# A retention whose carried state drops its padding and sits on four quarters of the array, with the first weight fetched a unit later

## The chip, the cores and the metric

One core of one Trainium2 chip runs the whole program. The metric is the device time of one execution in microseconds (us). The kernel before takes 575.39 us, the median of 3 runs (574.91 to 575.91). Everything is float32 in the results; the matrix products of the two MLPs are made of float32r pieces.

## The reference

Retention over 2 batches, 8 heads, 768 tokens and 64 columns a head, in blocks of 64 tokens with a state that decays; its result (1536 tokens by 512) goes through two MLPs of 512 to 2048 to 512, the first with a squared ReLU, the second with a leaky one. The weights come as 64-bit floats.

```
for b in range(nb):
    intra = (qb @ kb.T * Dmask) @ vb
    inter = (qb * lam_pow) @ kv_state
    out[sl] = intra + inter
    kv_state = lam_block * kv_state + (kb * rev_pow).T @ vb
h = np.maximum(x @ w_in, 0.0);  x = (h * h) @ w_out
h = x @ w_in2;  out = np.maximum(0.01 * h, h) @ w_out2
```

## The kernel before, in words

**Retention.** It works in units of 128 tokens: 2 batches of 6 chunks make 12 units, numbered 0 to 11. The 8 heads are 4 pairs p of two heads (par 0 and 1). A unit has these steps. `transposes` turns k and q by TensorE (L294), and ScalarE copies them out as kT and qT (L298). `scale_q` makes qS on VectorE (L304). `scores` multiplies kT by qT on the two row halves of the array, par 0 into one bank and par 1 into another (L311). `mask` multiplies with the decay table into Pm (L316). `state` scales k on GpSimd to kd (L329), multiplies by v (L335) and adds the old state times its decay (L342 on GpSimd, L347 on VectorE). `output` adds qS times the old state (L360) and Pm times v (L362) in one bank, and `split` takes this apart into xhi (ScalarE, L68) and xlo (VectorE, L69), the MLP's input. The tile of the state is 128 by 4 by 128: the two heads of a pair are two 64 by 64 blocks on the diagonal, with zeros beside them, so L360 contracts over 128 rows and writes 64.

**Order.** In this part the orders of TensorE and of SP, which issues the loads, are as the code is written; the scheduler places the other engines' work. The loop at the end of `retention` does for unit i: transposes of unit i+2, loads of k and q of unit i+4 and of v of unit i+2, then state and output of i, mask of i+1, scores of i+2. k has 5 buffers, q and v have 3 each.

**Weights.** A piece of weights (1 MB of 64-bit numbers, tile raw) is fetched by `fetch` and turned into float32r hi and lo in steps by `converting`: one on ScalarE (L114, the absolute value of the high words), the others on VectorE, to w1h (ScalarE, L135) and w1l (VectorE, L137). The first is fetched at i = 1 and converted one step in each of units 3 to 9.

**MLPs.** Four stages each, 64 us to the end. Two stages of the first MLP, (0,1) and (0,2), have their second layer for two token tiles as seven products instead of eight (`second_pair`, L503 in the profile like all products of the MLPs). Parts of it, P1, P6 and P67, are kept in DRAM by `keep`: written by SP in stage (0,1), added by GpSimd's DMAs in stage (0,2). After stage (0,2), ten DMAs from DRAM to DRAM (L684) add them up into `spill`, which the last stage reads.

Of the kernel before, what the change touches and what calls it, by code (L numbers as in the profile page):

```python
# [15 lines left out]
P = 128  # L16
# [3 lines left out]
def tile_retention_then_two_mlps(  # L20
# [43 lines left out]
    def dma(dst, src):  # L64
        return nc.sync.dma_start(dst, src)  # L65
# [7 lines left out]
    def source(l, s, n, h):  # L73
        w = ((w1, w2), (w3, w4))[l][n]
        if n == 0:
            return w[:, s * FS + h * CW:s * FS + (h + 1) * CW].rearrange("(k p) f -> p k f", p=P)
        return w[s * FS + h * CW:s * FS + (h + 1) * CW, :].rearrange("(k p) f -> p k f", p=P)

    order = [(0, 0, 0, 0), (0, 0, 0, 1), (0, 0, 1, 0), (0, 0, 1, 1)]
    stages = [(l, s) for l in range(2) for s in range(NS)]  # L80
    for before, stage in zip(stages, stages[1:]):
# [8 lines left out]
    def fetch():  # L90
        if todo:
            key = todo.pop(0)
            r = raw.tile([P, 4 * CW], I64, tag="raw", name="raw")
            k = 4 if key[2] == 0 else 2
            dma(r.rearrange("p (k f) -> p k f", k=k), source(*key))
            fetched.append((key, r))

    def converting():
# [85 lines left out]
    def retention(ctx_att, att):  # L184
# [90 lines left out]
                DTr[:, par], bass.AP(tensor=row.tensor, offset=row.offset, ap=[[1, P], [2 * W, NP], [1, C]])))  # L275

        def column_of_powers():
            ps = bank()[:, 0:H]
            nc.tensor.transpose(ps, pw[:, 1:C + 1], ident[0:H, 0:H])
            nc.scalar.copy(kdec, ps)  # L280

# [35 lines left out]

        st = []
        for e in range(2):
            st.append(att.tile([P, NP, P], F32, name=f"st{e}"))  # L320
            nc.gpsimd.memset(st[e], 0.0)

        def state(n):
            b, c = units[n]
            if c == NCH - 1:
                return
            kn, vn = nats[n, "k"], nats[n, "v"]
            kd = wk.tile([P, NP, 2, D], F32, tag="kd", name="kd")
            nc.gpsimd.tensor_tensor(  # L329
                out=kd, in0=kn.rearrange("s (a r) d -> s a r d", r=2),  # L330
                in1=kdec.rearrange("s (a r o) -> s a r o", r=2, o=1).to_broadcast([P, NP, 2, D]), op=ALU.mult)
            ps = bank()[:, 0:NP * D].rearrange("p (a e) -> p a e", a=NP)
            for p in range(NP):
                for par in range(2):
                    nc.tensor.matmul(ps[par * D:(par + 1) * D, p, :], kd[:, p, par, :], vn[:, 2 * p + par, :],  # L335
                                     start=True, stop=True)
            old, new = st[c % 2], st[(c + 1) % 2]
            if c:
                tmp = wk.tile([P, NP, D], F32, tag="tmp", name="tmp")
                for par in range(2):  # L340
                    r = slice(par * D, (par + 1) * D)
                    nc.gpsimd.tensor_tensor(out=tmp[r], in0=old[r, :, r],  # L342
                                            in1=LR[r, :, C - 1:C].to_broadcast([D, NP, D]), op=ALU.mult)
            for par in range(2):
                r = slice(par * D, (par + 1) * D)
                if c:
                    nc.vector.tensor_tensor(out=new[r, :, r], in0=ps[r], in1=tmp[r], op=ALU.add)  # L347
                else:
                    nc.vector.tensor_copy(new[r, :, r], ps[r])

        def output(n):
            b, c = units[n]
            vn = nats[n, "v"]
            ps = bank().rearrange("p (a s) -> p a s", a=NP)
            for p in range(NP):

                rows = [slice(par * D, (par + 1) * D) for par in range(2)]
                if c:
                    for r in rows:
                        nc.tensor.matmul(ps[r, p, :], st[c % 2][:, p, r], qS[n][:, p, :], start=True, stop=False)  # L360
                for par, r in enumerate(rows):
                    nc.tensor.matmul(ps[r, p, :], vn[:, 2 * p + par, :], Pm[n][:, par, p, :], start=c == 0, stop=True)  # L362
            t, o = divmod(b * S + c * C, TT)
            if xhi[t] is None:
                new_x(t)
            split(xhi[t][:, :, o:o + C], xlo[t][:, :, o:o + C], ps)

        n_units = len(units)
        FILL = TT // C
# [11 lines left out]
        rows_of_powers()  # L381
        scale_q(1, q1)
        scores(1)
        state(0)
        mask(0)
        output(0)
        scale_q(2, transposes(2))
        state(1)
        mask(1)
        scores(2)  # L390
        for i in range(n_units):
            if i and i + 2 < n_units:
                scale_q(i + 2, transposes(i + 2))
            if i + 4 < n_units:
                load(i + 4, "kq")
            if i + 2 < n_units:
                load(i + 2, "v")
            if i in (1, 9):
                fetch()
            if i:  # L400
                if i > 1:
                    state(i)
                output(i)
                if i + 1 < n_units:
                    mask(i + 1)
                if i + 2 < n_units:
                    scores(i + 2)
            if 3 <= i <= 9:
                convert(pin=True)


# [190 lines left out]
            put(h, r22[h], r22[h], 1, 1)  # L602
            put(h, s2[h], s2[h], 0, 1)

    partial = [{n: dram.tile([P, TT], F32, name=f"partial{p}{n}") for n in ("P1", "P6", "P67")} for p in range(2)]

    def keep(src, dst, first):
        f = plain()
# [6 lines left out]


    def second_pair(s):
        begun = (0, s - 1) in seven
        (g0h, g0l), (g1h, g1l) = g[0], g[1]
        x = {  # L620
            "B11": [(g0h[:, 2 * h], g0l[:, 2 * h]) for h in range(2)],
            "B21": [(g0h[:, 2 * h + 1], g0l[:, 2 * h + 1]) for h in range(2)],
            "B22": [(g1h[:, 2 * h + 1], g1l[:, 2 * h + 1]) for h in range(2)],
            "T1": [(g1h[:, 2 * h], g1l[:, 2 * h]) for h in range(2)],
            "T2": [(tt[2][:, 0, h], tt[2][:, 1, h]) for h in range(2)],
        }
        ps = {}

        def product(p, where, a, b, start=True):
            if start:  # L630
                ps[p, where] = bank()
            ops = []
            for h in range(2):
                if a[0] == "A":
                    i, j = int(a[1]) - 1, int(a[2]) - 1
                    hi, lo = (w[:, j, (2 * p + i) * P:(2 * p + i + 1) * P] for w in wts[0, s, 1, h])
                else:
                    hi, lo = (sums[0, s, 1, h][:, part, int(a[1]) - 1, p] for part in range(2))
                bh, bl = x[b][h]
                ops += [(hi, bh), (hi, bl), (lo, bh)]  # L640
            three(ps[p, where], ops, start, True, not start)
            return ps[p, where]

        def kept(p, i, k):
            return spill[0][k][2 * p + i]

        def late_split(n, old, m):
            x[n] = x[old]
            with tc.high_priority(offset=400):
                for h in range(2):  # L650
                    split(*x[n][h], later[m(h)])

        both = range(2)
        for p in both:
            keep(product(p, "A", "A11", "B11"), partial[p]["P1"], not begun)
            yield True
        for p in both:
            keep(product(p, "C", "S1", "T1"), kept(p, 1, 1), False)
            yield True
        late_split("T3", "T1", lambda h: (1, 2 * h))  # L660
        for p in both:
            keep(product(p, "A", "A12", "B21", False), kept(p, 0, 0), False)
            yield True
        late_split("T4", "B21", lambda h: (0, 2 * h + 1))
        for p in both:
            keep(product(p, "C", "S4", "B22", False), kept(p, 0, 1), False)
            yield True
        for p in both:
            keep(product(p, "B", "S2", "T2"), partial[p]["P6"], not begun)
            yield True  # L670
        for p in both:
            keep(product(p, "D", "A22", "T4"), kept(p, 1, 0), False)
            yield True
        yield from first(0, s, 2)
        for p in both:
            keep(product(p, "B", "S3", "T3", False), partial[p]["P67"], not begun)
            yield True
        opened.add(("sums", 0, s + 1))
        if (0, s + 1) not in seven:
            for p in both:  # L680
                p1, p6, p67 = (partial[p][n] for n in ("P1", "P6", "P67"))
                for dst, src in ((p67, p1), (kept(p, 0, 1), p1), (kept(p, 0, 1), p6), (kept(p, 1, 0), p67),
                                 (kept(p, 1, 1), p67)):
                    nc.gpsimd.dma_start(dst, src, accum_op=ALU.add, max_dma_last_dim=TT)  # L684

    def second(l, s, t, ms=range(4)):
        last = s == NS - 1
# [94 lines left out]
```

## Time and profile before

| what | us |
|---|---|
| median of 3 runs | 575.39 |
| the profiled execution, whole | 576.42 |
| its span, first to last instruction | 574.5 |
| TensorE busy in the span | 564.2 |
| VectorE busy | 418.4 |
| ScalarE busy | 305.0 |
| GpSimd busy | 83.9 |

The profiled execution took 1.92 us outside the span, and 1.03 us more than the median. Retention fills the first 64 us, the MLPs the rest. TensorE's orders are written out, so its idle time is what an order or a neighbour costs. All rows name the kernel's lines.

### The profile page before, as it was taken

Reading aid. Unit: us, or ns where it says so; the run is one execution under the profiler, and the core shown is the slowest. Engines: PE = TensorE matmul, PEld = TensorE weight load, DVE = VectorE, ACT = ScalarE, POOL = GpSimd, SP = SyncE. Lnnn points to the kernel's source line nnn. Section 1 sums busy time; section 2 is a strip of 40 time slices with the busy share of each in tenths; the row PEclk is TensorE's granted clock in tenths of the full one; section 3 lists DMA queues with packets and bytes.
Section 4 is the critical chain, followed back from the end, with each engine's and each line's share of the span. In section 5 each row is a group of like instructions: output and inputs, shape, how many; then the busy total and the mean of one; then the engine's idle time right before and its main releaser. Section 6 shows DMA issues by size and latency. Waiting matters only on the chain.

```text
span 574.5 us, 8051 instructions
## 1 busy us (share of the span) xinstructions
PE 564.2 (98%) x3075; PEld 470.7 (82%) x3075; DVE 418.4 (73%) x589; ACT 305.0 (53%) x477; POOL 83.9 (15%) x101
## 2 busy tenths in 40 slices
PE   7989999999999999999999999999999999999997
PEld 6878888888788888888888888888888888888886
DVE  3879999999927599498478999929873996217222
ACT  2344598546757687758448374553562376225110
POOL 3426000000040105445000000000203011310000
PEclk9999999999999999999999999999999999999999
DMA  8997434665492649999713216341529523661432
GB/s 172 239 213 177 156 121 138 234 183 180 172 164 57 73 148 181 203 249 189 185 36 91 76 41 216 128 165 74 103 55 246 109 29 47 76 90 56 162 113 92
DMA packets 74071, 78.12 MB, mean 136 GB/s; under 512 B 40105, under 2 KB 46513, under 8 KB 74033
## 3 DMA queue, kind: packets, MB, share of 16 engines
q1 hardware_dynamic: 60448, 60.57, 34.6%
q0 software_dynamic: 13056, 16.78, 20.9%
q8 instruction: 24, 0.39, 0.3%
q10 hardware_dynamic: 528, 0.26, 0.2%
q14 instruction: 15, 0.11, 0.1%
HBM read 52.43 MB, written 27.80 MB: 140 GB/s over the span
## 4 chain that ended last, share of the span: by engine, by line
PE 74%; DVE 15%; DMA 6%; issue 3%; SPq 1%; ACT 1%; POOL 0%; DVEq 0%; POOLq 0%; ACTq 0%
PE ps L503 72%; DMA raw<-in_moe_w_in 2%; DVE rb L122 2%; DMA raw<-in_moe_w_out 2%; DVE hb L125 2%; DVE hb L118 2%; SPq L65 1%; DVE rb L121 1%; DVE hb L115 1%; DVE Pm L316 1%; DMA k<-in_k 1%; DVE xlo L69 1%; DVE w1l L137 0%; DVE g1l L474 0%; DVE sw L442 0%
## 5 line engine op out<-in xcount | busy, mean ns | idle before, releaser
L503 PE MATMUL ps<-xhi,w1h 128*128 128x512 f32 x288 | 112.1, 389 | 0.0
L503 PE MATMUL ps<-xlo,w1h 128*128 128x512 f32 x288 | 112.0, 389 | 0.0
L503 PE MATMUL ps<-xhi,w1l 128*128 128x512 f32 x288 | 112.0, 389 | 0.0
L613 POOL DMA_DIRECT2D spill<-f x48 | 46.9, 1047 | 347.6 <-ACT f L609 347.5
L609 ACT COPY f<-ps 128x512 f32<-128x512 f32 x84 | 48.9, 586 | 74.1 <-PE ps L503 72.7
L503 PEld LDWEIGHTS ps<-xhi,w1h 128*128 128x128 f32 x288 | 54.1, 188 | 11.3 <-issue 0.2
L503 PEld LDWEIGHTS ps<-xlo,w1h 128*128 128x128 f32 x288 | 54.1, 188 | 11.3
L503 PEld LDWEIGHTS ps<-xhi,w1l 128*128 128x128 f32 x288 | 54.1, 188 | 11.2
L474 DVE TENSOR_TENSOR g0l<-f,g0h 128x512 fp32r<-128x512 f32 x52 | 35.1, 687 | 33.7 <-ACT f L470 22.1
L503 PE MATMUL ps<-w2l,g0h 128*128 128x512 f32 (+1 forms) x132 | 50.5, 383 | 0.0
L503 PE MATMUL ps<-w2h,g0l 128*128 128x512 f32 (+1 forms) x132 | 50.5, 383 | 0.0
L503 PE MATMUL ps<-w2h,g0h 128*128 128x512 f32 (+1 forms) x132 | 50.5, 383 | 0.0
L137 DVE TENSOR_TENSOR w2l<-hb,w2h 128x1024 fp32r<-128x1024 f32 x16 | 19.5, 1222 | 39.8 <-ACT w2h L135 39.8
L114 ACT ACTIVATE hb<-raw 128x1024 f32<-128x1024 f32 x32 | 36.8, 1150 | 19.2 <-DVE w2l L137 7.4
L503 PE MATMUL ps<-g0h,w2h 128*128 128x512 f32 x104 | 40.5, 389 | 0.0
L503 PE MATMUL ps<-g0l,w2h 128*128 128x512 f32 x104 | 40.5, 389 | 0.0
L503 PE MATMUL ps<-g0h,w2l 128*128 128x512 f32 x104 | 40.5, 389 | 0.0
L122 DVE SCALAR_TENSOR_TENSOR rb<-raw,rb 128x1024 f32<-128x1024 uint32 x32 | 39.1, 1221 | 0.4
L125 DVE TENSOR_TENSOR hb<-hb,rb 128x1024 f32<-128x1024 f32 x32 | 39.1, 1220 | 0.4
L118 DVE SCALAR_TENSOR_TENSOR hb<-raw,hb 128x1024 uint32<-128x1024 uint32 x32 | 39.1, 1220 | 0.3
L567 DVE TENSOR_TENSOR f<-ps,f 128x512 f32<-128x512 f32 x40 | 26.2, 684 | 9.9 <-PE ps L503 9.9
L714 DVE TENSOR_TENSOR f<-ps,f 128x512 f32<-128x512 f32 (+1 forms) x25 | 16.7, 669 | 22.9 <-PE ps L503 21.7
(141 smaller groups left out, 1139.4 us busy)
## 6 DMA issues: line engine op xcount, KB each, us to landing
raw<-in_moe_w_in SPq DMA_DIRECT2D x16, 1024.0 KB, 5.6
raw<-in_moe_w_out SPq DMA_DIRECT2D x16, 1024.0 KB, 5.0
spill<-f POOLq DMA_DIRECT2D x48, 256.0 KB, 4.8
spill<-f SPq DMA_DIRECT2D x24, 256.0 KB, 2.6
f<-spill SPq DMA_DIRECT2D x24, 256.0 KB, 2.9
k<-in_k SPq DMA_DIRECT2D x12, 256.0 KB, 4.9
q<-in_q SPq DMA_DIRECT2D x12, 256.0 KB, 5.1
v<-in_v SPq DMA_DIRECT2D x12, 256.0 KB, 4.8
```

The costliest lines, as they stand in the source:

```text
L65: return nc.sync.dma_start(dst, src)
L114: nc.scalar.activation(hf, w_hi.bitcast(F32), AF.Abs)
L118: yield ve.scalar_tensor_tensor(out=hb, in0=w_hi, scalar=0xC0000000, in1=hb, op0=ALU.bitwise_and, op1=ALU.bitwise_or)
L122: yield ve.scalar_tensor_tensor(out=rf, in0=w_lo, scalar=2.0 ** -52, in1=rf, op0=ALU.mult, op1=ALU.mult)
L125: yield ve.tensor_tensor(out=hf, in0=hf, in1=rf, op=ALU.add)
L137: yield ve.tensor_tensor(out=lo, in0=hf, in1=hi, op=ALU.subtract)
L474: nc.vector.tensor_tensor(out=glo, in0=r, in1=ghi, op=ALU.subtract)
L503: nc.tensor.matmul(ps, a, b, start=start and n == 0, stop=stop and n == len(ops) - 1, skip_group_check=again)
L567: ve.tensor_tensor(out=out, in0=ps[h, where], in1=other, op=ALU.add)
L609: nc.scalar.copy(f, src)
L613: nc.gpsimd.dma_start(dst, f, accum_op=ALU.add)
L714: nc.vector.tensor_tensor(out=a, in0=ps, in1=a, op=ALU.add)
```

## The change

Four parts. **State:** the tile is 128 by 4 by 64, without zeros. The product with qS is 64 by 64 for each head on one quarter of the array, row half par and column half par, or the other column half for odd pairs. All eight go first, then the eight of Pm and v. The two banks of one output hold pairs 0 and 2, and pairs 1 and 3, and the split is made in two parts. In odd pairs the two heads come out with their halves swapped, so the odd blocks of w_in's rows are fetched with swapped halves: 8 of the pieces by three DMAs instead of one. GpSimd's tmp and VectorE's st are one instruction of 128 partitions, and two memsets go. **Weights:** the first piece is fetched at i = 2, converted in units 4 to 9, with two steps in 9. **Head:** mask(0) stands ahead of state(0), k's transposes of unit 2 ahead of output(0), and the column of powers is transposed into the idle bank. **Partial results:** each of the two stages has its own P1, P6 and P67, all written by SP (six additions by GpSimd become writes), and ten DRAM to DRAM additions follow each stage.

```diff
+            if key[0] or key[2]:
+                dma(dst, src)
+            else:
+                dma(dst[:, 0:k:2], src[:, 0:k:2])
+                for a, b in ((half[0], half[1]), (half[1], half[0])):
+                    dma(dst[a, 1:k:2], src[b, 1:k:2])
...
-            st.append(att.tile([P, NP, P], F32, name=f"st{e}"))
-            nc.gpsimd.memset(st[e], 0.0)
+            st.append(att.tile([P, NP, D], F32, name=f"st{e}"))
...
+                nc.gpsimd.tensor_tensor(out=tmp, in0=old, in1=LR[:, :, C - 1:C].to_broadcast([P, NP, D]), op=ALU.mult)
+                nc.vector.tensor_tensor(out=new, in0=ps, in1=tmp, op=ALU.add)
...
+            ps = [bank()[:, 0:2 * C].rearrange("p (a s) -> p a s", a=2) for _ in range(2)]
+            heads = [(p, par ^ p % 2) for p in range(NP) for par in range(2)]
+            def place(p, par):
+                return ps[p % 2][half[par ^ p % 2], p // 2, :]
+            if c:
+                for p, par in heads:
+                    nc.tensor.matmul(place(p, par), st[c % 2][half[par], p, :], qS[n][half[par], p, :],
+                                     start=p < 2, stop=False, skip_group_check=True)
+            for p, par in heads:
+                nc.tensor.matmul(place(p, par), vn[:, 2 * p + par, :], Pm[n][:, par, p, :],
...
+            for e in range(2):
+                split(xhi[t][:, e::2, o:o + C], xlo[t][:, e::2, o:o + C], ps[e])
...
+        mask(0)
         state(0)
-        mask(0)
+        transposes(2, "k")
         output(0)
-        scale_q(2, transposes(2))
+        scale_q(2, transposes(2, "q"))
...
-            if i in (1, 9):
+            if i in (2, 9):
                 fetch()
...
-            if 3 <= i <= 9:
+            for _ in range((i in range(4, 10)) + (i == 9)):
                 convert(pin=True)
...
-            keep(product(p, "B", "S2", "T2"), partial[p]["P6"], not begun)
+            keep(product(p, "B", "S2", "T2"), partial[p]["P6"], True)
...
-        if (0, s + 1) not in seven:
-            for p in both:
...
+        for p in both:
+            p1, p6, p67 = (partial[p][n] for n in ("P1", "P6", "P67"))
+            for dst, src in ((p67, p1), (kept(p, 0, 1), p1), (kept(p, 0, 1), p6), (kept(p, 1, 0), p67),
+                             (kept(p, 1, 1), p67)):
+                nc.gpsimd.dma_start(dst, src, accum_op=ALU.add, max_dma_last_dim=TT)
```

TensorE in one unit, before: k's and q's transposes (L294), state (L335), output as pairs of two matmuls in turn (L360 with the state, L362 with v), then the scores (L311).

```order
L294 MATMUL ps<-ident,q 128x128 x4
L335 MATMUL ps<-v,kd 64x64 x8
L360 MATMUL ps<-qS,st_168 64x128 x2
L362 MATMUL ps<-Pm,v 64x128 x2
L360 MATMUL ps<-qS,st_168 64x128 x2
L362 MATMUL ps<-Pm,v 64x128 x2
L360 MATMUL ps<-qS,st_168 64x128 x2
L362 MATMUL ps<-Pm,v 64x128 x2
L360 MATMUL ps<-qS,st_168 64x128 x2
L362 MATMUL ps<-Pm,v 64x128 x2
L311 MATMUL ps<-qT,kT 128x128 x8
```

The same unit in the changed kernel, whose line numbers are some ten higher:

```order
L303 MATMUL ps<-ident,q 128x128 x4
L343 MATMUL ps<-v,kd 64x64 x8
L364 MATMUL ps<-qS,st_168 64x128 x8
L367 MATMUL ps<-Pm,v 64x128 x8
L320 MATMUL ps<-qT,kT 128x128 x8
```

The same number of matmuls stands there; the eight of the state are now together, ahead of the eight of v.

ScalarE in units 2 to 4, before, where L114 is the first step of the first weight piece, kT and qT (L298) what TensorE's scores read, and xhi (L68) the output's high half:

```order
L298 COPY kT<-ps 128x512
L298 COPY qT<-ps 128x512
L68 CAST xhi_278<-ps 128x4x128
L114 ACTIVATE hb<-raw 128x1024
L298 COPY kT<-ps 128x512
L298 COPY qT<-ps 128x512
L68 CAST xhi_278<-ps 128x4x128
```

The same engine in the changed kernel, from the same xhi on to the weight step:

```order
L68 CAST xhi_282<-ps 128x2x128 x2
L307 COPY kT<-ps 128x512
L307 COPY qT<-ps 128x512
L68 CAST xhi_282<-ps 128x2x128 x2
L307 COPY kT<-ps 128x512
L307 COPY qT<-ps 128x512
L123 ACTIVATE hb<-raw 128x1024
L68 CAST xhi_585<-ps 128x2x128 x2
```

The step on raw has moved behind the next unit's kT and qT, and behind those of the unit after, ahead of the xhi of unit 4.

VectorE at the end of retention, before, from the mask of unit 10 (the first L316) to the first step of the next weight piece (L115):

```order
L316 TENSOR_TENSOR Pm<-ps,DTr 128x512 x2
L137 TENSOR_TENSOR w1l_928<-hb,w1h_927 128x1024
L304 TENSOR_TENSOR qS<-ps,LR 128x512
L347 TENSOR_TENSOR st_168<-ps,tmp 64x4x64 x2
L69 TENSOR_TENSOR xlo_842<-ps,xhi_841 128x4x128
L316 TENSOR_TENSOR Pm<-ps,DTr 128x512 x2
L347 TENSOR_TENSOR st_170<-ps,tmp 64x4x64 x2
L115 TENSOR_SCALAR hb<-hb 128x1024
```

The same stretch in the changed kernel:

```order
L325 TENSOR_TENSOR Pm<-ps,DTr 128x512 x2
L134 TENSOR_TENSOR hb<-hb,rb 128x1024
L313 TENSOR_TENSOR qS<-ps,LR 128x512
L349 TENSOR_TENSOR st_168<-ps,tmp 128x256
L146 TENSOR_TENSOR w1l_943<-hb,w1h_942 128x1024
L69 TENSOR_TENSOR xlo_851<-ps,xhi_850 128x2x128 x2
L325 TENSOR_TENSOR Pm<-ps,DTr 128x512
L349 TENSOR_TENSOR st_169<-ps,tmp 128x256
L325 TENSOR_TENSOR Pm<-ps,DTr 128x512
L69 TENSOR_TENSOR xlo_851<-ps,xhi_850 128x2x128 x2
L124 TENSOR_SCALAR hb<-hb 128x1024
```

Two long steps of the weight piece stand behind the mask of unit 10 instead of one, and each update of st is one instruction.

## Rows read from the trace of the kernel before

**Rows 1.** The page, part 1: busy us, share of the span, instructions.
```profile
PE 564.2 (98%) x3075; PEld 470.7 (82%) x3075; DVE 418.4 (73%) x589; ACT 305.0 (53%) x477; POOL 83.9 (15%) x101
```
**Rows 2.** Waits of TensorE: total us, times, longest.
```profile
PE ps L335 <- issue: 2.5, 1, 2.5
PE ps L311 <- ACT qT L298: 2.2, 3, 1.8
PE ps L220 <- POOL pw L225: 1.5, 1, 1.5
PE ps L503 <- DVE g1l L69: 0.5, 1, 0.5
PE ps L294 <- DMA q<-in_q: 0.2, 1, 0.2
```
**Rows 3.** Timeline of TensorE: start, us, what, [idle before, releaser].
```profile
32.73 0.94 PE L311 MATMUL ps<-qT,kT 64*128 64x128 f32 x12 [1.76 <-ACT qT L298]
```
**Rows 4.** Timeline of ScalarE, the same stretch.
```profile
30.60 1.12 ACT L114 ACTIVATE hb<-raw 128x1024 f32<-128x1024 f32 x1 [3.47 <-DMA raw<-in_moe_w_in]
32.09 0.59 ACT L298 COPY qT<-ps 128x512 f32<-128x512 f32 x1
```
**Rows 5.** Timeline of SP's queue: the issue of raw, of v of unit 6.
```profile
22.76 1.13 SPq L65 DMA_DIRECT2D raw<-in_moe_w_in  x1
...
36.07 1.06 SPq L65 DMA_DIRECT2D v<-in_v  x1
```
**Rows 6.** Timeline of TensorE, one unit, scores to scores.
```profile
49.31 1.16 PE L311 MATMUL ps<-qT,kT 64*128 64x128 f32 x16
50.41 0.66 PE L294 MATMUL ps<-ident,k 128*128 128x128 f32 x4
50.90 0.60 PE L294 MATMUL ps<-ident,q 128*128 128x128 f32 x4
51.43 0.69 PE L335 MATMUL ps<-v,kd 128*64 128x64 f32 x16
51.95 0.39 PE L360 MATMUL ps<-qS,st 128*64 128x128 f32 x4
...
53.48 0.39 PE L362 MATMUL ps<-Pm,v 128*64 128x128 f32 x4
53.79 0.60 PE L311 MATMUL ps<-qT,kT 64*128 64x128 f32 x6
```
**Rows 7.** Windows: busy us of each engine, PEclk, DMA share, GB/s.
```profile
34.00:61.00 27.00, 27.00 (x438) 24.25 (x439) 26.20 (x44) 11.81 (x20) 11.94 (x14) 1.00 0.96 223
40.00:52.00 12.00, 12.00 (x194) 10.62 (x192) 11.63 (x19) 4.88 (x10) 5.71 (x6) 1.00 1.07 214
52.00:54.00 2.00, 2.00 (x38) 1.83 (x36) 2.00 (x4) 0.89 (x2) 1.74 (x1) 1.00 0.06 14
```
**Rows 8.** Tile v, 0 to 62 us: from issue to landing.
```profile
DMA to landing us min/median/max: 2.9/4.8/7.9
```
**Rows 9.** Timeline of TensorE: the state of unit 6.
```profile
43.34 0.69 PE L335 MATMUL ps<-v,kd 128*64 128x64 f32 x16
```
**Rows 10.** Lines of VectorE, 34 to 61 us: busy us, mean ns.
```profile
L69 DVE TENSOR_TENSOR xlo<-ps,xhi 128x512 fp32r<-128x512 f32 x7 | 4.8, 692 | 0.6 <-ACT xhi L68 0.5
...
L347 DVE TENSOR_TENSOR st<-ps,tmp 64x256 f32<-64x256 f32 x9 | 3.8, 418 | 0.2
```
**Rows 11.** Timeline of VectorE at the end of retention.
```profile
56.71 1.22 DVE L137 TENSOR_TENSOR w1l<-hb,w1h 128x1024 fp32r<-128x1024 f32 x1
...
61.15 0.86 DVE L347 TENSOR_TENSOR st<-ps,tmp 64x256 f32<-64x256 f32 x2
```
**Rows 12.** Timeline of TensorE in stage (0,1).
```profile
155.44 0.50 PE L503 MATMUL ps<-g1l,sw 128*128 128x512 f32 x1 [0.53 <-DVE g1l L69]
```
**Rows 13.** Timeline of VectorE at the head.
```profile
13.27 1.29 DVE L316 TENSOR_TENSOR Pm<-ps,DTr 128x512 f32<-128x512 f32 x2 [6.79 <-DMA DTr<-tab]
```
**Rows 14.** Timeline of GpSimd after stage (0,2): the first addition.
```profile
234.07 1.06 POOL L684 DMA_DIRECT2D spill<-partial0P  x1 [5.75 <-DMA spill<-f]
```

More of the change, by code (lines that the diff above doesn't have):

```diff
@@ L77, in source @@
         return w[s * FS + h * CW:s * FS + (h + 1) * CW, :].rearrange("(k p) f -> p k f", p=P)
+    half = [slice(e * D, (e + 1) * D) for e in range(2)]
     order = [(0, 0, 0, 0), (0, 0, 0, 1), (0, 0, 1, 0), (0, 0, 1, 1)]
@@ L94, in fetch @@
             k = 4 if key[2] == 0 else 2
-            dma(r.rearrange("p (k f) -> p k f", k=k), source(*key))
+            dst, src = r.rearrange("p (k f) -> p k f", k=k), source(*key)
+            if key[0] or key[2]:
[4 more added lines that the diff above has]
+                    dma(dst[a, 1:k:2], src[b, 1:k:2])
             fetched.append((key, r))
@@ L277, in column_of_powers @@
         def column_of_powers():
-            ps = bank()[:, 0:H]
+            ps = idle[:, P:P + H]
             nc.tensor.transpose(ps, pw[:, 1:C + 1], ident[0:H, 0:H])
@@ L339, in state @@
                 tmp = wk.tile([P, NP, D], F32, tag="tmp", name="tmp")
[L340 to L349, printed above, removed]
+                nc.gpsimd.tensor_tensor(out=tmp, in0=old, in1=LR[:, :, C - 1:C].to_broadcast([P, NP, D]), op=ALU.mult)
+                nc.vector.tensor_tensor(out=new, in0=ps, in1=tmp, op=ALU.add)
+            else:
+                nc.vector.tensor_copy(new, ps)
         def output(n):
@@ L353, in output @@
             vn = nats[n, "v"]
[L354 to L362, printed above, removed]
+            ps = [bank()[:, 0:2 * C].rearrange("p (a s) -> p a s", a=2) for _ in range(2)]
[8 more added lines that the diff above has]
+                nc.tensor.matmul(place(p, par), vn[:, 2 * p + par, :], Pm[n][:, par, p, :],
+                                 start=c == 0, stop=True, skip_group_check=True)
             t, o = divmod(b * S + c * C, TT)
@@ L365, in output @@
                 new_x(t)
-            split(xhi[t][:, :, o:o + C], xlo[t][:, :, o:o + C], ps)
+            for e in range(2):
+                split(xhi[t][:, e::2, o:o + C], xlo[t][:, e::2, o:o + C], ps[e])
         n_units = len(units)
@@ L603, in first_pair @@
             put(h, s2[h], s2[h], 0, 1)
-    partial = [{n: dram.tile([P, TT], F32, name=f"partial{p}{n}") for n in ("P1", "P6", "P67")} for p in range(2)]
+    partials = {
+        s: [{n: dram.tile([P, TT], F32, name=f"partial{s}{p}{n}") for n in ("P1", "P6", "P67")} for p in range(2)]
+        for _, s in seven
+    }
     def keep(src, dst, first):
@@ L617, in second_pair @@
     def second_pair(s):
-        begun = (0, s - 1) in seven
+        partial = partials[s]
         (g0h, g0l), (g1h, g1l) = g[0], g[1]
@@ L654, in second_pair @@
         for p in both:
-            keep(product(p, "A", "A11", "B11"), partial[p]["P1"], not begun)
+            keep(product(p, "A", "A11", "B11"), partial[p]["P1"], True)
             yield True
@@ L675, in second_pair @@
         for p in both:
-            keep(product(p, "B", "S3", "T3", False), partial[p]["P67"], not begun)
+            keep(product(p, "B", "S3", "T3", False), partial[p]["P67"], True)
             yield True
         opened.add(("sums", 0, s + 1))
-        if (0, s + 1) not in seven:
-            for p in both:
[L681 to L684, printed above, removed]
+        for p in both:
[3 more added lines that the diff above has]
+                nc.gpsimd.dma_start(dst, src, accum_op=ALU.add, max_dma_last_dim=TT)
     def second(l, s, t, ms=range(4)):
```

## The prediction

> **What bounds the kernel now.** I read the page's part on busy times first: TensorE works in 564.2 us of the 574.5 us span, 98% [rows 1], so a change pays only if it shortens TensorE's own work or one of its waits. Then its waits, which are five rows and 6.9 us in all [rows 2]: 2.5 us at the first state product, 2.2 us in which the scores wait for qT, 1.5 us at the very start, 0.5 us in an MLP, 0.2 us for a load of q. In the windows VectorE is as full as TensorE while retention runs (26.20 of 27 us, TensorE 27.00, ScalarE and GpSimd under 12), and the DMA engines' share there is about 1 [rows 7]. So two neighbours stand right behind TensorE in retention. The clock granted there was 1.00, the 2.4 GHz level.
>
> **First weight piece.** The longest of the waits for qT is 1.76 us, before the scores that start at 32.73 us [rows 3]. ScalarE had it: the first step on the raw piece stands ahead of the next kT and qT, idles 3.47 us for the piece's load, runs 1.12 us from 30.60 on, and only then copies qT, which starts at 32.09 us [rows 4]. The load was issued at 22.76 us [rows 5] and landed at about 30.6 us, 7.8 us later. In the changed order this step stands behind kT and qT of two more units (5 and 6), and the piece is issued behind the three loads that followed it, k and q of unit 6 and v of unit 4. At about 1.1 us an issue [rows 5] that is 3.3 us, and with 7.8 us again it lands at 34 us. The next scores behind the step are those of unit 7. Without the stall those of unit 5 start at 30.97 us; a unit is 4.48 us (scores at 49.31 and 53.79 us [rows 6]), and the one on the way without a state product 0.52 less, so those of unit 7 start at about 39.4. Ahead of them ScalarE has the step (1.12), a high half and two copies, some 0.6 each: the piece may land as late as 36.5 us, so there are 2.5 us of room. Its three DMAs carry the same 1 MB and cost SP two more issues, 2.2 us, ahead of loads that are wanted later. Gain 1.76 us. Bounds: nothing, if the wait only moves, to 1.8.
>
> The conversion's seven steps keep their number but end one step later. At the end of retention VectorE then has an addition and w1l behind the mask of unit 10 instead of w1l alone. Before, from w1l at 56.71 us to the end of the last state at 62.0 us are 5.3 us [rows 11]. The added long step costs about 1.2 us (w1l took 1.22), the two state updates give back 0.43 each, and the last state is placed between the last two masks. So the last mask comes about half a microsecond later against the mask of unit 10. TensorE's last output does not begin before the last state, whose place against that mask stays. I count it as nothing, with bounds 0 and 0.6.
>
> **State.** Eight groups of an output, each two matmuls side by side, start from 51.95 to 53.48 us, 0.219 us apart (1.53 over 7), and with two records a matmul that is 0.109 us for a round of two [rows 6]. On quarters four state matmuls go side by side, if the array lets them. Sixteen records are then 4 rounds, 0.44 us, where the state's four groups took 0.87: 0.44 saved. Against it stand changes of the array's shape. Before, state and output have one shape, 128 rows by 64 columns. Now there are two more changes, into quarters and out again. What one costs can be read at its two ends. After the last round of the output the scores start 0.31 us later, where 0.219 would do: 0.09 at the end of a shape. At the beginning, k's transposes take 0.49 us (50.41 to 50.90) where four rounds are 0.44, 0.05 more; the state products take 0.52 us for eight rounds of 64 columns that need 0.44, 0.08 more; the scores take 1.10 us to the next shape, where eight rounds and the 0.09 end need 0.97, 0.13 more. Two changes cost 2 x 0.09 and two beginnings of 0.05 to 0.13, so 0.28 to 0.44, and the unit gains 0.16 to 0. The quarters split the rows as the scores do (0.13), and the products with v have the form of the state products (0.08): 0.39, so 0.05 gained a unit. Ten units have a state term, hence 0.5 us, bounds 0 to 1.6 with the quarters really at work together.
>
> No row shows two row halves writing the same bank, since the scores put par 0 and par 1 in separate banks. The change does it: the two heads of pair 0 go to row halves 0 and 1, and to the two halves of one bank. The Trainium skill, "TensorEngine Tiling (Array Packing)", section Restrictions and Gotchas, says under PSUM pressure that different row tiles cannot access the same PSUM bank at the same time; no run here has tried it yet, and by that rule the first rival below would be the outcome.
>
> The other engines. VectorE's state update was 64 partitions twice at 418 ns [rows 10]; with 128 partitions it is one of the same 256 columns, 0.43 us less a unit. The low half's 692 ns [rows 10] becomes two of half the columns, between 0.35 and 0.43 us each, 0 to 0.2 more. In sum VectorE gets 0.2 to 0.4 us a unit of room, where it had 0.8 us in 27. ScalarE's high half is also split in two, some 0.2 us more a unit, with 11.81 us busy of 27 to hide it [rows 7]; its qT stands in front of TensorE's scores by over a microsecond. GpSimd's tmp becomes one instruction, and two memsets go while GpSimd waits for other things. None of this is on the path by itself.
>
> **Loads.** If retention runs 2 us earlier, the loads must as well. Their share is 1.07 from 40 to 52 us and then falls to 0.06 [rows 7], so the DMA engines work without a pause until the last load is in. v of unit 6 is issued at 36.07 us [rows 5] and lands 4.8 us later by the median [rows 8], at 40.9, and is used at 43.34 us [rows 9]. That is 2.4 us of room, of which some 2.0 would be used up: 1.76 plus a few twentieths. By the median it just holds, by the longest (7.9 us) it would not. I take 0.3 us given back, between 0 and 1.5.
>
> **Head.** The first state product waits 2.5 us [rows 2] since it writes to the bank that the first mask must have read, and that mask starts at 13.27 us, after 6.79 us for the decay table [rows 13]. The new order changes neither the bank nor the table. k's transposes of unit 2 are drawn ahead of output(0), but right behind it q's transposes waited for their load [rows 2], so what is won is lost there. 0, bounds -0.3 and +0.3.
>
> **Stage (0,1) and partial results.** In that stage TensorE waits 0.53 us for one low half on VectorE, at 155.44 us [rows 12]. VectorE was behind there by its conversions. Its stream up to that instruction gets shorter by about 1.8 us (ten state updates at 0.43 less the split low halves), more than that wait, so 0.5 goes, bounds 0 to 0.5. The additions from DRAM to DRAM after stage (0,2) ran on GpSimd from 234.07 us on [rows 14], with no wait of TensorE near them [rows 2]; ten more after stage (0,1), and six accumulations turned to writes, lie in a GpSimd that is busy 15% [rows 1]. Cover gone, a tile f that is set free late would hold up ScalarE, but its use is a few us off. 0, bounds 0 and +0.5.
>
> **Sum.** -1.76 - 0.5 + 0.3 - 0.5 = -2.46 us, on the profiled execution's own 576.42 us, 573.96. That execution is 1.03 us above the median of the runs, so against 575.39 us this is 572.9; I say 573.0 us.
>
> **Rivals.** First, the quarters don't run together. Two matmuls at once need 8 rounds, 0.87 us, as before, and the two changes of shape are pure loss: 0.39 a unit. If two row halves can't write one bank at once, the heads of a pair must follow each other, only neighbours of two pairs can overlap, and I count 5 groups or 10 rounds: another 0.22, 0.61 a unit. Ten units cost 3.9 to 6.1 us, less 1.76 and 0.5: 577.0 to 579.2 us, slower. It decides from a loss of 0.23 us a unit on. For it: no row of before shows that access. Against: the column halves run side by side without loss, and the scores' row halves too, in two banks.
>
> Second, the loads or the raw piece hold the gain: retention stays bound by DMA from 40 us on, or ScalarE waits for raw a unit later as it did before. Then of 1.76 only 0.3 remain, with 0.5 or nothing of the other terms: 574.1 to 575.1 us, say 574.6. For it speaks a share of 1.07; against it, 2.4 us of room at v.
>
> Third, the quarters begin without a slow first round: 0.18 for two changes, 0.26 gained a unit, 2.6 us, less 0.5 more to the loads: 571.3 us. Every beginning in the rows is slow, which speaks against it.
>
> **Chances.** Forecast 0.56 (its own range 572.0 to 574.1), first rival 0.13, second 0.18, third 0.10; 0.03 are left for the head and the end of retention. 0.2% of the time is 1.15 us, about what a measurement of this kernel tells from no change, so faster is below 574.24 us. Forecast and third rival, with a part of the second, make 0.70 faster; most of the second and the remainder make 0.17 the same; the first makes 0.13 slower. The range 571.2 to 575.8 us holds all but the first rival and some of the third.
>
> **What would show it.** Right: TensorE's wait for qT near 31 us is gone and none for raw or v stands in its place; state matmuls of a unit start 16 records within about 0.6 us, and from state product to scores it takes 2.3 us instead of 2.36; the 0.53 us wait in stage (0,1) is missing. Wrong: records of the quarters 0.109 us apart in pairs or singly, a new wait for k, q or v between 35 and 50 us, or one for an xlo or w1h at 61 to 64 us, or any wait for an f tile near 210 us.

## The result and the profile after

The changed kernel takes 579.70 us, the median of 9 runs (578.48 to 580.94); beside it the kernel before took 575.63. The ratio is 1.0056, with a 95% interval of 1.0042 to 1.0069: 0.56% slower, where 573.0 us was forecast (the two medians are 4.1 us, 0.7%, apart). The profiled execution took 579.77 us, with a span of 578.0 us.

The page's busy times answer to [rows 1]: TensorE works as long as before, within half a microsecond. Its units got shorter (below), but from 14 to 20 us its granted clock, the column behind the five engines' busy times, is 0.72, where the profiled execution of the kernel before has 1.00. The page's line of the changed kernel, and this window in the changed kernel and in the kernel before:

```profile
PE 564.7 (98%) x3075; PEld 467.4 (81%) x3075; DVE 415.4 (72%) x591; ACT 304.9 (53%) x489; POOL 82.6 (14%) x95
14.00:20.00 6.00, 6.00 (x66) 4.86 (x62) 4.33 (x9) 1.92 (x4) 3.03 (x4) 0.72 1.00 201
14.00:20.00 6.00, 5.54 (x80) 4.64 (x80) 5.88 (x12) 2.25 (x4) 3.75 (x5) 1.00 0.86 191
```

6.00 us at 0.72 are the work of 4.3 us at full clock, by estimate, where the kernel before did 5.5. The 1.2 us between them are about what ten shorter units save.

Of the 3.5 us that the span grew by, 3.0 are idle time, and TensorE's waits say where (us in total, times, longest; [rows 2] before):

```profile
PE ps L343 <- issue: 2.0, 1, 2.0
PE ps L511 <- DVE g1l L69: 2.0, 2, 1.3
PE ps L511 <- ACT g1h L68: 1.8, 2, 1.3
PE ps L229 <- POOL pw L234: 1.5, 1, 1.5
PE ps L303 <- DMA k<-in_k: 1.1, 1, 1.1
PE ps L303 <- DMA q<-in_q: 0.5, 1, 0.5
PE ps L343 <- DMA v<-in_v: 0.4, 1, 0.4
PE ps L320 <- ACT qT L307: 0.2, 1, 0.2
PE ps L364 <- DVE st L349: 0.2, 1, 0.2
```

The wait for qT is down from 2.2 to 0.2 us. In its place stand 2.0 us for k, q and v, and the waits in the MLPs have grown from 0.5 to 3.8 us. The four of them, in TensorE's timeline, are in stage (0,1) and in stage (0,2):

```profile
154.41 0.51 PE L511 MATMUL ps<-g1h,sw 128*128 128x512 f32 x1 [0.48 <-ACT g1h L68]
156.23 0.51 PE L511 MATMUL ps<-g1l,sw 128*128 128x512 f32 x1 [1.31 <-DVE g1l L69]
...
220.18 0.51 PE L511 MATMUL ps<-g1h,sw 128*128 128x512 f32 x1 [1.31 <-ACT g1h L68]
221.33 0.50 PE L511 MATMUL ps<-g1l,sw 128*128 128x512 f32 x1 [0.65 <-DVE g1l L69]
```

The first product of the MLPs starts at 63.20 us, 0.75 ahead of the 63.95 us of the kernel before. By 156 us the changed kernel is 0.78 behind, by 222 us 3.3, and it stays there. Retention gains little, and two stages of the first MLP lose 4.1 us.

TensorE in one unit (answers to [rows 6]) is the part that got faster:

```profile
49.25 1.16 PE L320 MATMUL ps<-qT,kT 64*128 64x128 f32 x16
50.34 0.66 PE L303 MATMUL ps<-ident,k 128*128 128x128 f32 x4
50.84 0.60 PE L303 MATMUL ps<-ident,q 128*128 128x128 f32 x4
51.37 0.69 PE L343 MATMUL ps<-v,kd 128*64 128x64 f32 x16
51.98 0.67 PE L364 MATMUL ps<-qS,st 64*64 64x128 f32 x16
52.58 1.09 PE L367 MATMUL ps<-Pm,v 128*64 128x128 f32 x16
53.60 1.16 PE L320 MATMUL ps<-qT,kT 64*128 64x128 f32 x16
```

Scores to scores are 4.35 us where they were 4.48. The quarters (L364) take 0.60 us to the next shape. Two matmuls at a time would need 0.87 for the rounds alone; four at a time need 0.44 and leave 0.16 for the changes of shape. So four do run together, though the heads of a pair write from two row halves into one bank. The rule of the Trainium skill that different row tiles cannot access one bank at the same time ("TensorEngine Tiling (Array Packing)", Restrictions and Gotchas) does not show in this trace, where the two write different partitions of the bank.

What the conversion waits for is in ScalarE's group of first steps (busy us and mean ns, then idle us before them with releasers):

```profile
L123 ACT ACTIVATE hb<-raw 128x1024 f32<-128x1024 f32 x32 | 36.8, 1149 | 26.9 <-DMA raw<-in_moe_w_in 11.7 <-DMA raw<-in_moe_w_out 6.6 <-DVE w2l L146 6.4
```

In the kernel before the same group idles 19.2 us, 5.5 of it for w_in. Eight of its sixteen pieces are those that now come in three loads. Their issues in SP's timeline, for one piece in the MLP and with stores between:

```profile
120.85 0.38 SPq L65 DMA_DIRECT2D raw<-in_moe_w_in  x1
121.28 0.46 SPq L65 DMA_DIRECT2D spill<-f  x1
121.79 0.61 SPq L65 DMA_DIRECT2D raw<-in_moe_w_in  x1
122.50 0.57 SPq L65 DMA_DIRECT2D spill<-f  x1
123.11 0.61 SPq L65 DMA_DIRECT2D raw<-in_moe_w_in  x1
```

The third is issued 2.3 us after the first. And a smaller load is not there sooner. Over the whole kernel the page gives, from issue to landing (KB each, median us; the first line is the kernel before):

```profile
raw<-in_moe_w_in SPq DMA_DIRECT2D x16, 1024.0 KB, 5.6
raw<-in_moe_w_in SPq DMA_DIRECT2D x8, 512.0 KB, 5.7
raw<-in_moe_w_in SPq DMA_DIRECT2D x16, 256.0 KB, 5.9
```

A piece is there when its last load is, so the later issue is not made up for. That is the place to look.

### The profile page after: what moved, and what is told of

Same layout as the page of the kernel before. It is cut to its first block, busy times and chain, and to the rows that moved or that the text cites. A ratio compares the mean times of both kernels' runs of the same rounds, so it can differ in the third digit from the quotient of the medians.

```text
span 578.0 us, 8085 instructions
## 1 busy us (share of the span) xinstructions
PE 564.7 (98%) x3075; PEld 467.4 (81%) x3075; DVE 415.4 (72%) x591; ACT 304.9 (53%) x489; POOL 82.6 (14%) x95
## 4 chain that ended last, share of the span: by engine, by line
PE 74%; DVE 12%; DMA 7%; ACT 3%; issue 2%; SPq 1%; POOL 0%; DVEq 0%; POOLq 0%; ACTq 0%
PE ps L511 69%; DMA raw<-in_moe_w_in 3%; DMA raw<-in_moe_w_out 2%; DVE rb L131 2%; DVE hb L127 2%; DMA q<-in_q 1%; DVE hb L134 1%; PE ps L303 1%; PE ps L367 1%; SPq L65 1%; DVE hb L124 1%; DMA v<-in_v 1%; DVE rb L130 1%; PE ps L320 1%; DVE w2l L146 1%
## 5 line engine op out<-in xcount | busy, mean ns | idle before, releaser
L123 ACT ACTIVATE hb<-raw 128x1024 f32<-128x1024 f32 x32 | 36.8, 1149 | 26.9 <-DMA raw<-in_moe_w_in 11.7
```

The costliest lines, as they stand in the source:

```text
L123: nc.scalar.activation(hf, w_hi.bitcast(F32), AF.Abs)
```

## The experiments

The kernel before was timed anew beside each group of four kernels, since its median moves by some tenths. Each ratio is against the one beside it: 576.18 us for the first four below (partial results, one load, first piece, head), 576.05 for four others (three loads in the later pieces only, the two versions with loads a unit apart, the piece moved alone) and 576.45 for the rest. Lines of an edit that are left out are marked with three dots.

**One change undone at a time.** Partial results as before (P1, P6 and P67 shared again, additions after stage (0,2) only):

```diff
-            keep(product(p, "A", "A11", "B11"), partial[p]["P1"], True)
+            keep(product(p, "A", "A11", "B11"), partial[p]["P1"], not begun)
...
```

> The changed kernel with the partial results as before (P1, P6, P67 shared by the two stages, GpSimd adds them, ten DRAM to DRAM additions after stage (0,2) only). Theory one: the additions after stage (0,1) hold up the weight piece that ScalarE waits for at 211 us, and with it the 2.5 us that the changed kernel loses between 218 and 222 us; without them the raw wait of 4.1 us goes and the time falls from 579.7 to about 577.2 us. Rival: the weights' conversion is late for another reason (its later start), so the loss at 218 to 222 us stays and the time is 579 to 580 us.

580.3 us, ratio 1.0075 (1.0051 to 1.0098). The time does not bear theory one out. The wait at 220 us goes, and TensorE waits 1.6 us for an f tile before a product at 226.40 us instead: ScalarE's copy into that tile waits 2.93 us for the DMA that adds to the shared partial result. In the profiled execution the MLPs do take 2.35 us less than in the changed kernel (from 64.55 us to the end at 577.0), but retention takes 1.35 more, with a wait of 2.7 us for k, although nothing in retention was changed. So one execution's wait for a load is not a price by itself.

One load for every piece:

```diff
-            if key[0] or key[2]:
+            if True:
                 dma(dst, src)
...
```

> The changed kernel with each weight piece fetched by one DMA; the swap of halves in the odd blocks is left out, so the weights' rows there are in the wrong order. Theory one: three DMAs land about 2 us later than one, each conversion starts when its piece has landed, and the delay adds up to the waits at 154 to 156 us; with one DMA TensorE loses about 1.5 us less there, 578.2 us. Rival: the conversion's later start (a unit later) is what makes these waits; then nothing changes, 579.7 us.

574.67 us, ratio 0.9972 (0.9957 to 0.9986). This version leaves the swap of halves out, so it gives a price and is no kernel to use. All of the loss goes, three times what was expected. Its waits of TensorE are these, with none for k, q, v or g1h left:

```profile
PE ps L343 <- issue: 1.8, 1, 1.8
PE ps L229 <- POOL pw L234: 1.5, 1, 1.5
PE ps L511 <- DVE g1l L69: 0.8, 1, 0.8
PE ps L320 <- ACT qT L307: 0.2, 1, 0.2
PE ps L364 <- DVE st L349: 0.2, 1, 0.2
```

Its MLPs begin 3.51 us earlier than before's, against 0.75 in the changed kernel, and it keeps 3.3 of them to the end. The granted clock from 14 to 20 us is 0.72 here too, so the head's clock is not what sets the two apart. ScalarE's wait for w_in is 4.7 us.

The first piece at i = 1 again:

```diff
-            if i in (2, 9):
+            if i in (1, 9):
-            for _ in range((i in range(4, 10)) + (i == 9)):
+            if 3 <= i <= 9:
```

> The changed kernel with the first weight piece fetched at i = 1 again and converted in units 3 to 9. Theory one: the 1.76 us wait for qT comes back near 31 us and the waits for k and q at 37 to 39 us (1.7 us) go; the MLP's waits stay: 579.2 to 580.2 us. Rival: the later start makes the MLP's waits, so they go too and the time is about 576.5 us.

579.52 us, ratio 1.0069 (1.0044 to 1.0093): no change, as theory one had it. It missed in how: the wait for qT did not come back (0.2 us), and the one for k did not go (1.1 us).

The head as before:

```diff
-        mask(0)
         state(0)
-        transposes(2, "k")
+        mask(0)
         output(0)
-        scale_q(2, transposes(2, "q"))
+        scale_q(2, transposes(2))
...
```

> The changed kernel with the head's order as before (state(0), mask(0), output(0), both transposes of unit 2; the column of powers in its own bank). Theory one: the granted clock's fall between 14 and 18 us (0.72 in that window) comes from the new order of the first products, and goes with it: 0.5 to 1.2 us less, about 578.8 us. Rival: the clock falls there whatever the order, or the head costs nothing: 579.7 us.

578.79 us, ratio 1.0045 (1.0025 to 1.0064), inside the changed kernel's interval. In the window from 14 to 20 us the granted clock is 0.80, where the changed kernel has 0.72. The fall doesn't come from the order alone: with the old order it is there, and with the new one the run with the partial results as before has 1.00 in this window. The mean clock of the kernel before's own executions lies between 0.993 and 1.000 too. The head is not told apart from nothing.

**Three loads in the kernel before**, in straight order, nothing else:

```diff
-            dma(r.rearrange("p (k f) -> p k f", k=k), source(*key))
+            dst, src = r.rearrange("p (k f) -> p k f", k=k), source(*key)
+            if key[0] or key[2]:
+                dma(dst, src)
+            else:
+                dma(dst[:, 0:k:2], src[:, 0:k:2])
+                for a in (slice(0, D), slice(D, P)):
+                    dma(dst[a, 1:k:2], src[a, 1:k:2])
```

> The kernel before with the pieces of the first MLP's first layer fetched by three DMAs, in the straight order of halves. Theory one: three DMAs land later whatever they carry where; loads of q and k wait in retention and conversions come late in stages (0,1) and (0,2): 3 to 5 us slower, 579 to 581 us. Rival: it is the crossing of the halves, or the changed kernel's shorter units, that matters, and three straight DMAs cost nothing in the kernel before: 576 us.

582.18 us, ratio 1.0096 (1.0072 to 1.0121): 5.7 us slower. The cost needs neither the swap nor the quarters. The profiled execution is the slowest of the six (584.97 us). TensorE's waits that are new or longer there:

```profile
PE ps L509 <- ACT f L615: 1.6, 1, 1.6
...
PE ps L509 <- DVE g1l L69: 1.3, 1, 1.3
PE ps L509 <- DVE g0l L480: 1.2, 1, 1.2
PE ps L341 <- DMA v<-in_v: 1.1, 1, 1.1
PE ps L509 <- ACT g1h L68: 1.0, 1, 1.0
```

The wait for qT is down to 0.2 us, although the piece is still fetched at i = 1. ScalarE's step on raw, at 31.97 us, now stands behind the kT and qT of the next unit (28.73 and 29.21), where it stood ahead of them [rows 4]: with three loads the scheduler has written another order.

**Three loads in the six later pieces only:**

```diff
-            if key[0] or key[2]:
+            if key[0] or key[2] or not key[1]:
                 dma(dst, src)
```

> The changed kernel with one load a piece in the first stage (two pieces; the swap is left out there, so those weights' rows are in the wrong order) and three loads in the six later pieces. Theory one: of the 5 us that three loads cost, the part in retention (2.8 us: its start of the MLPs against the kernel with one load everywhere) goes, and the MLP's part stays: 576.5 to 577.5 us. Rival: the lateness at 154 and 220 us is inherited from the first pieces; then it goes too, 574.7 us.

578.74 us, ratio 1.0048 (1.0031 to 1.0064), against 574.67 with one load everywhere. Four of the five microseconds stay, so most of the loss is the MLP's own and not inherited: the lead is 2.18 us at the start of the MLPs and is lost at 154 and 219 us. Two to three were expected to stay. That lead is 1.3 us under the one with one load everywhere, with pieces that come alike up to there; the clock from 14 to 20 us is 0.55 in this execution, against 0.72. More goes to TensorE's clock behind the waits. Windows of this kernel (length, busy us of TensorE, its loads, VectorE, ScalarE, GpSimd, then the granted clock, DMA share, GB/s):

```profile
218.00:220.00 2.00, 0.49 (x1) 0.19 (x1) 2.00 (x4) 1.54 (x3) 0.00 (x0) 1.00 0.00 0
220.00:222.00 2.00, 1.74 (x5) 1.45 (x6) 2.00 (x4) 2.00 (x5) 0.00 (x0) 0.70 0.23 86
222.00:224.00 2.00, 2.00 (x6) 1.52 (x6) 2.00 (x3) 1.16 (x3) 0.86 (x1) 0.50 0.87 186
224.00:226.00 2.00, 2.00 (x10) 1.61 (x9) 2.00 (x4) 1.91 (x4) 0.28 (x1) 0.95 0.93 313
```

After waits of 2.4 and 0.7 us it falls to half, 1.2 GHz, and six products run in a window that otherwise holds ten.

**Ways around the three loads.** With one load, and the halves swapped back when the output is split:

```diff
...
-            for e in range(2):
-                split(xhi[t][:, e::2, o:o + C], xlo[t][:, e::2, o:o + C], ps[e])
+            split(xhi[t][:, 0::2, o:o + C], xlo[t][:, 0::2, o:o + C], ps[0])
+            for a, b in ((half[0], half[1]), (half[1], half[0])):
+                split(xhi[t][a, 1::2, o:o + C], xlo[t][a, 1::2, o:o + C], ps[1][b])
```

> The changed kernel with one DMA for every weight piece; the halves of the odd pairs are swapped back in the split of the output (two instructions on 64 partitions each on ScalarE and VectorE instead of one on 128), so the weights' rows stay in their order. Theory one, now that one load a piece took 5 us off: three DMAs a piece are what the changed kernel loses by; here 574.7 to 575.5 us, since the split's extra instructions lie beside TensorE's work. Rival: VectorE, already full in retention, becomes the bound through the extra 0.35 us a unit: 577 us or more.

582.14 us, ratio 1.0097 (1.0070 to 1.0125). The rival holds: TensorE waits 3.4 us for VectorE's state and starts the MLPs 2.20 us late. That lateness again makes waits at 154 us (g1h 1.6, g1l 1.3), although each piece comes in one load. It points to the lateness of the stream of conversions as what decides there, and to loads as one way to make it late. The same with all else as before:

> As e5, with the first weight piece, the head and the partial results as before: the state on four quarters alone. Theory one: the unit is 0.13 us shorter, ten times, and the 1.76 us wait near 31 us stays: 574.5 to 575.2 us. Rival: the shorter units run into the loads, which leave nothing of it: 576 us.

580.27 us, ratio 1.0065 (1.0047 to 1.0083). Neither theory had this, since the split's cost on VectorE was taken for nothing again: TensorE waits 3.0 us for qT and 1.7 for VectorE's state there.

Two loads a piece, with heads 0 to 3 in one column half and 4 to 7 in the other:

```diff
-                dma(dst[:, 0:k:2], src[:, 0:k:2])
-                for a, b in ((half[0], half[1]), (half[1], half[0])):
-                    dma(dst[a, 1:k:2], src[b, 1:k:2])
+                src = src.rearrange("(c k d) f -> c d k f", c=2, k=k)
+                for c in range(2):
+                    dma(dst[half[c]], src[c])
...
```

(`src` is here the columns of w_in as they lie in memory.)

> The changed kernel with another place for each head: heads 0 to 3 in column half 0 and heads 4 to 7 in column half 1, so that a weight piece comes by two DMAs of 64 partitions instead of three. Theory one: the loss goes with the number of DMAs beyond one, so about half of the 5 us stays: 577 us. Rival: any DMA of 64 partitions is what is slow, and two of them are no better than three: 579 to 580 us.

575.52 us, ratio 0.9983 (0.9971 to 0.9995). Neither theory had it: the loss does not go by the number of loads, and loads of 64 partitions are not slow as such. This version beats both kernels, by 0.17%, which the interval only just tells from nothing, and by some 0.7%. Its profiled execution is the slowest of the twelve (577.73 us), and in it the first product of the MLPs starts at 65.14 us, later than before's 63.95. Its first piece still holds up the next loads:

```profile
PE ps L304 <- DMA k<-in_k: 2.3, 1, 2.3
...
PE ps L304 <- DMA q<-in_q: 0.7, 1, 0.7
PE ps L512 <- DVE g1l L69: 0.6, 1, 0.6
```

In the MLPs it loses nothing at 154 us and 0.9 us at 219. ScalarE waits 5.9 us for w_in, about as in the kernel before (5.5).

The first piece's two loads a unit apart:

```diff
-            if i in (2, 9):
-                fetch()
+            if i in (1, 2):
+                fetch((i - 1,))
...
```

> As the version with two loads a piece, with the first piece's two loads issued a unit apart (at i = 1 and i = 2) instead of together. Theory one: the first piece takes the DMA engines for some 3 us in one go and k and q of the next unit come 3.0 us late; in two portions the loads catch up between them, 1.5 to 3 us less: 572.5 to 574 us. Rival: retention is bound by the bytes it loads, wherever the piece stands, and the waits only move: 575.5 us.

575.89 us, ratio 0.9995 (0.9986 to 1.0004). The rival: the wait for k shrinks to 0.4 us and one of 1.9 us for v appears, behind which the granted clock is 0.53 and 0.62 from 36 to 40 us. The MLPs start at 64.51 us, not ahead of before's.

The same with the partial results as before:

> The version with two loads a unit apart, with the partial results as before. Theory one: the additions after stage (0,1) delay the next weight piece by a few us and cost 0.5 to 1 us at 218 us: as much faster than with them. Rival: they cost nothing once the pieces come in time: no difference between the two.

576.99 us, ratio 1.0021 (1.0007 to 1.0034), apart from the 0.9995 of the kernel it differs from. The new partial results are worth about 1.1 us here, where theory one had them cost and the rival had no difference. What goes with them is two waits, for an f tile (0.9 us) and g0l (1.2 us), which this kernel has and the other doesn't.

**The piece moved alone**, in the kernel before (the inverse of the edit of the run with the first piece at i = 1):

> The kernel before with the first weight piece fetched at i = 2 and converted in units 4 to 9, nothing else. Theory one: with one load a piece the 1.76 us wait for qT goes and no wait for loads takes its place: 574.3 to 575 us against 576.4 of the kernel before. Rival: the loads behind the piece are late by as much: 576.4 us.

576.32 us, ratio 1.0004 (0.9994 to 1.0015). The rival's number came out and its reason did not: no wait for k or v stands in place of the one for qT, and the one for q is 0.4 us, 0.2 before. The lead is lost at the end of retention. TensorE's last scores there, its waits behind them and the first product of the MLPs:

```profile
56.32 1.16 PE L311 MATMUL ps<-qT,kT 64*128 64x128 f32 x16
61.27 0.78 PE L360 MATMUL ps<-qS,st 128*64 128x128 f32 x3 [1.00 <-DVE st L347]
62.45 0.32 PE L362 MATMUL ps<-Pm,v 128*64 128x128 f32 x1 [0.28 <-DVE Pm L316]
64.12 0.50 PE L503 MATMUL ps<-xhi,w1h 128*128 128x512 f32 x1
```

The same scores and the same product in the kernel before:

```profile
58.27 1.16 PE L311 MATMUL ps<-qT,kT 64*128 64x128 f32 x16
63.95 0.50 PE L503 MATMUL ps<-xhi,w1h 128*128 128x512 f32 x1
```

A lead of 1.95 us at the scores is 0.17 behind at the product.

## Why the prediction was wrong, point by point

**The step that failed** is in the part on the first weight piece: "Its three DMAs carry the same 1 MB and cost SP two more issues, 2.2 us, ahead of loads that are wanted later." It took bytes for the price of a load, looked at one piece of eight, and had no term for the other seven. Taken away they give 5.0 us back (574.67 against 579.70, not timed side by side), put alone into the kernel before they cost 5.7. Without them the predicted gain is of the right sign: with one load a piece, and the swap left out, the change is 1.6 us faster than before (ratio 0.9957 to 0.9986), where 2.4 was forecast.

**The stall.** That the wait for qT goes was right. But the -1.76 us were not to be had by the move alone: in the kernel before the lead lasts until the last scores and is then lost on VectorE, to the state update and the mask (1.00 and 0.28 us of waiting). I had read VectorE as full [rows 7] and still counted the end of retention as nothing, with 0.6 at most. With one load and the lighter state update these waits are down to 0.2 us, and retention gains 3.51 us. With three loads, the first is issued at 26.97 us instead of the 26.1 that I worked out, with 2.58 us for the issue of v ahead of it where I took 1.1, and the piece is waited for until 35.83 us instead of 34 (32.34 with one load). k and q behind it come late:

```profile
37.52 0.63 PE L303 MATMUL ps<-ident,k 128*128 128x128 f32 x4 [1.15 <-DMA k<-in_k]
38.69 0.63 PE L303 MATMUL ps<-ident,q 128*128 128x128 f32 x4 [0.54 <-DMA q<-in_q]
```

These 1.7 us are the mechanism of the second rival, to which I gave 0.18. The term for the loads was 0.3 us, with 1.5 at most; it measured 2.0 here (1.1 for k, 0.5 for q, 0.4 for v).

**The state on quarters.** The mechanism and sign were right, the size too small: 0.13 us a unit, where I chose 0.05 out of 0 to 0.16. The first rival, slower by quarters that don't run together, is out. It alone had forecast a slower kernel; the kernel became slower by a mechanism that no rival had.

**The wait in stage (0,1)** was to go; it grew from 0.53 to 1.8 us, and stage (0,2) got 2.0 of its own. I had counted VectorE's instructions ahead of it and not when the data of its conversions land.

**The partial results** are not told apart from nothing in the changed kernel, as forecast; in the run where it could be told they gave about 1 us. **The head** was forecast to be nothing. Undoing it gives a ratio of 1.0045 against 1.0056, with intervals that overlap, so it is open at the level of a microsecond. The prediction had no term for the granted clock, which fell there in some executions and not in others.

**What stays open.** Three loads also change the orders that the scheduler writes, as ScalarE's step on raw showed in the kernel before with three loads. How much of the 4 us in the MLPs is late landing, and how much the other order, no run separates. That the landing is late is shown by ScalarE's 11.7 us of waiting for w_in, against 5.5 before and 4.7 with one load. Why two loads a piece cost under a microsecond against one, and three some 5, is open too.

## What to carry to other kernels

Count the loads and their issues, not the bytes alone, and do so for every piece that a changed source line fetches, to the end of the kernel. Where a stream of conversions feeds engines with fixed orders, a late piece can come out far behind as one late operand that stops TensorE. A stall that is moved away is worth its length only if the next neighbours, read one by one, have that much room.

## What the runs showed of the hardware that was not expected

Four 64 by 64 products ran together on the quarters, with row halves 0 and 1 writing into different partitions of the same bank: 0.60 us for sixteen records, from the first to the next shape. And a wait can cost more than its length: after 2.4 and 0.7 us of idling TensorE was granted 0.50, its lower level, for a window of 2 us, while after waits of 1.31 and 0.65 us at the same place in the changed kernel it stayed at 1.00. The longest wait alone doesn't sort the cases: in the run with the head as before it fell to 0.59 between 156 and 158 us, after waits of 0.8 and 1.3 us.
